# Eighty-four products of zeros behind the last result of an attention and Fourier kernel

## The chip, the core and the metric

The kernel runs on one core of a Trainium2 chip. A core has five engines with queues of their own: TensorE (PE; its weight loads are listed apart as PEld), VectorE (DVE), ScalarE (ACT), GpSimd (POOL) and SyncE (SP), which here issues nearly all transfers between memory and the on-chip buffer. Each queue runs in order, and the engines wait for each other by semaphores. The metric is the device time of one execution in microseconds (us). Before the change the median of three runs is 2921.22 us (2918.11 to 2922.79).

## The reference

Two independent results are put side by side in the columns of one output of 2048 x 2048 numbers.

```python
# A: attention with 32 heads of 32 columns, S = 2048, D = 1024
q, k, v = split(x @ wqkv)
p = softmax(q @ k.T * Dh ** -0.5)
a = concat_heads(p @ v) @ wo
# B: Fourier mixing, the real part of a transform along both axes
ar, ai = x @ dft_hid_re.T, x @ dft_hid_im.T
b = dft_seq_re @ ar - dft_seq_im @ ai
return concatenate([a, b], axis=-1)
```

## The kernel before

The work is cut into products of 128 x 128 weights (the stationary operand) with 512 moving columns, each into one bank of PSUM. Most operands are split into a rounded part and a remainder, and a product of two such operands is three TensorE products in fp32r; the function `group` emits them (line 414). Both results use fast matrix multiplication in two levels of seven products, so that many operands are sums of blocks, made by VectorE and GpSimd.

TensorE's program is one long interleaved order. A planner, class `Plan`, keeps a model of each engine's time. The closing loop of the kernel (lines 2054 to 2129) walks along the plan and picks, for each free moment of TensorE, among three streams of the attention (S: scores, line 1853; T: transposed scores, line 1975; V: products with the values, line 1994) and a list of "fills" (line 414: the projections of queries, keys and values, the Fourier transform, the output projection). `pl.others()` emits what the other engines do in between. A second loop (lines 2130 to 2135) emits what is left for the other engines once TensorE's list is empty. All of it stands under a guard (`guard`, line 2052) that keeps the engines' orders as they are emitted. So what is emitted behind that second loop stands behind everything else on its engine.

The last piece of work is `project_end` and `total` (lines 1440 to 1483): for each of 16 row blocks and two column halves, six products (two blocks of `wo`, three products each) are added by VectorE (line 1474) to a sum that was loaded from memory (line 1455) and is stored as a part of the output (line 1479). The very last store is split in two, one half on SyncE's queue and one on ScalarE's. The sums of a row block stand in a slot of the pool `big`: eight slots, taken in turn, so that row block 11 uses slot 0, and block 15 the slot that block 7 had. Slot 1 holds one of the four pieces of `wo`.

Buffers that the change uses: the slots of `big` (4 KB in each of 128 partitions, one buffer per slot), the tag "c" of the pool `pre` (three buffers of 2 KB, last used for blocks that are loaded to be added), and `psS` (two PSUM tiles of two banks each, used for the scores in line 1853). A tile that is taken again waits for the readers and writers of the tile that had its place. Eight products of zeros already stand at the start of the kernel (lines 376 to 379), ahead of the first loads.

Of the kernel before, what the change touches and what calls it, by code (L numbers as in the profile page):

```python
# [8 lines left out]
F32 = mybir.dt.float32  # L9
F32R = mybir.dt.float32r  # L10
# [6 lines left out]
P = 128  # L17
# [6 lines left out]
NB = 512  # L24
# [198 lines left out]
def kernel(  # L223
# [12 lines left out]
    nc = tc.nc  # L236
# [35 lines left out]
    big = ctx.enter_context(tc.tile_pool(name="big", bufs=1, side="right"))  # L272
# [13 lines left out]
    pre = ctx.enter_context(tc.tile_pool(name="pre", bufs=1, reuse_waits="tile"))  # L286
# [34 lines left out]
    psS, psT, psD = (pools[n] for n in ("psS", "psT", "psD"))  # L321
# [1486 lines left out]
    def op_pool():  # L1808
        if "op" not in late:
            att().release()  # L1810
            qk0.release()
            late["atl"].release()
            late["oph"] = ctx.enter_context(tc.tile_pool(name="oph", bufs=1, side="right", reuse_waits="tile"))
            late["op"] = ctx.enter_context(tc.tile_pool(name="op", bufs=1, reuse_waits="tile"))
        return late["op"]
# [238 lines left out]
    while nf < len(fills) or any(place[n] < len(s) for n, s in streams.items()):  # L2054
# [59 lines left out]
        if ok:  # L2114
            n = min(ok)[1]
# [14 lines left out]
    while True:  # L2130
        pl.others()
        t = pl.next_time()
        if t > 1e17:
            break
        pl.now = max(t, pl.now + 1e-3)
    guard.__exit__(None, None, None)
    op_pool()

# [27 lines left out]
```

## Time and profile before

| | us |
|---|---|
| median of three runs | 2921.22 |
| lowest, highest | 2918.11, 2922.79 |
| the profiled execution | 2929.45 |
| its span, first to last instruction | 2927.7 |

The granted TensorE clock of that execution is 0.999 of full speed. In the views below, times in a timeline count from the span's start: start, duration, engine, line, operation, output<-inputs and the number of instructions merged in a row. In a group, "x8" is the number of instructions, then come busy time, the mean time of one in nanoseconds, and the idle time of the engine just before them with what ended it. A TensorE product's own time reaches from its first column to the last result, so that products that follow each other overlap; the distance of their starts is the pace. In a table of stages the columns are the stretch, the summed time, busy time and number of instructions of PE, PEld, DVE, ACT and POOL, the granted clock, the share of the 16 DMA engines' time, and GB/s. "SPq" and "PEldq" are the sequencers of these engines: waits, issues and drains.

### The profile page before, as it was taken

Reading aid. Unit: us, or ns where it says so; the run is one execution under the profiler, and the core shown is the slowest. Engines: PE = TensorE matmul, PEld = TensorE weight load, DVE = VectorE, ACT = ScalarE, POOL = GpSimd, SP = SyncE. Lnnn points to the kernel's source line nnn. Section 1 sums busy time; section 2 is a strip of 40 time slices with the busy share of each in tenths; the row PEclk is TensorE's granted clock in tenths of the full one; section 3 lists DMA queues with packets and bytes.
Section 4 is the critical chain, followed back from the end, with each engine's and each line's share of the span. In section 5 each row is a group of like instructions: output and inputs, shape, how many; then the busy total and the mean of one; then the engine's idle time right before and its main releaser. Section 6 shows DMA issues by size and latency. Waiting matters only on the chain.

```text
span 2927.7 us, 47039 instructions
## 1 busy us (share of the span) xinstructions
PE 2904.0 (99%) x14728; PEld 2107.2 (72%) x14728; DVE 2386.5 (82%) x3251; ACT 2373.3 (81%) x4509; POOL 1241.3 (42%) x975
## 2 busy tenths in 40 slices
PE   9999999999999999999999999999999999999999
PEld 8887776777667777777676677667667777777777
DVE  7679888788788887788888898888988788788745
ACT  5348898888888888988999898898889888888741
POOL 2325534142233433337655456666675352243200
PEclk9999999999999999999999999999999999999999
DMA  9989978697789988867899776887876665677558
GB/s 345 349 298 328 314 225 272 222 346 269 268 289 339 309 297 287 291 213 218 291 348 333 226 223 216 276 272 229 271 229 208 204 180 181 193 246 226 188 191 287
DMA packets 485844, 768.18 MB, mean 262 GB/s; under 512 B 120382, under 2 KB 153406, under 8 KB 485470
## 3 DMA queue, kind: packets, MB, share of 16 engines
q1 hardware_dynamic: 485452, 765.04, 79.4%
q8 instruction: 119, 1.95, 0.3%
q14 instruction: 129, 1.06, 0.1%
q10 hardware_dynamic: 144, 0.13, 0.0%
HBM read 511.74 MB, written 253.25 MB: 261 GB/s over the span
## 4 chain that ended last, share of the span: by engine, by line
PE 75%; DMA 4%; DVE 1%; ACT 1%; SPq 0%; issue 0%; POOL 0%; DVEq 0%; ACTq 0%; POOLq 0%
PE pd L414 34%; PE psT L1975 14%; PE pd L1994 13%; PE psS L1853 13%; PE psT L414 2%; ACT psS L1862 1%; DVE negm L1859 1%; DMA qs<-m_d 1%; DMA slot<-in_ct 0%; DMA g<-in_ct 0%; DMA hl<-ha_d 0%; ACT pt L1979 0%; DMA m_d<-lt 0%; DMA ha_d<-slot 0%; DMA g<-g_d 0%
## 5 line engine op out<-in xcount | busy, mean ns | idle before, releaser
L414 PE MATMUL pd<-slot,hl 128*128 128x512 f32 x5028 | 1446.7, 390 | 4.2 <-DMA hl<-ha_d 1.4
L1979 ACT ACTIVATE pt<-psT 128x512 f32<-128x512 f32 x2048 | 1191.5, 668 | 260.7 <-PE psT L1975 258.5
L1859 DVE TENSOR_REDUCE negm<-psS 128x1 f32<-128x1024 f32 x1024 | 1240.7, 1221 | 198.3 <-PE psS L1853 190.1
L1862 ACT ACTIVATE psS<-psS,negm 128x1024 f32<-128x1024 f32 x1024 | 1189.2, 1161 | 47.4 <-DVE negm L1859 44.5
L414 PEld LDWEIGHTS pd<-slot,hl 128*128 128x128 f32 x5028 | 943.6, 188 | 204.8 <-DVE negm L1859 2.7
L1975 PE MATMUL psT<-qs,ks 128*128 128x512 f32 x2048 | 802.4, 395 | 4.4 <-DMA qs<-m_d 3.2
L1975 PEld LDWEIGHTS psT<-qs,ks 128*128 128x128 f32 x2048 | 382.2, 188 | 160.0 <-issue 53.0
L1853 PE MATMUL psS<-ks,qs 128*128 128x512 f32 x1552 | 473.1, 391 | 4.2 <-ACT psS L1862 4.2
L1994 PE MATMUL pd<-pt,vt 128*32 128x512 f32 x4096 | 460.9, 596 | 1.2 <-DVE e L723 0.9
L1853 PEld LDWEIGHTS psS<-ks,qs 128*128 128x128 f32 x1552 | 289.5, 188 | 69.1 <-ACT psS L1862 11.0
L504 POOL TENSOR_TENSOR slot<-raw,slot 128x512 fp32r<-128x512 f32 x153 | 196.2, 1291 | 316.1 <-DVE slot L501 116.6
L1994 PEld LDWEIGHTS pd<-pt,vt 128*32 128x32 f32 x4096 | 123.4, 110 | 285.1 <-issue 268.3
L504 POOL TENSOR_TENSOR slot<-slot,slot 128x512 fp32r<-128x512 f32 x183 | 234.3, 1292 | 206.1 <-DVE slot L501 54.5
L1862 ACT ACTIVATION_READ_ACCUMULATOR psS<-psS,negm 128x1 f32 x1024 | 287.0, 280 | 0.0
L504 POOL TENSOR_TENSOR hl<-raw,hl 128x512 fp32r<-128x512 f32 x122 | 156.8, 1289 | 257.4 <-DVE hl L501 84.7
L479 POOL TENSOR_TENSOR raw<-raw,g 128x512 f32<-128x512 f32 x119 | 153.3, 1291 | 226.6 <-ACT pt L1979 31.3
L414 PE MATMUL pd<-slot,slot 128*128 128x512 f32 x780 | 210.6, 389 | 0.1
L414 PEld LDWEIGHTS pd<-slot,slot 128*128 128x128 f32 x780 | 146.4, 188 | 30.9 <-DVE e L723 0.4
L1853 PE MATMUL psS<-ks,qx 128*128 128x512 f32 x496 | 151.0, 394 | 3.3 <-ACT psS L1862 3.2
L479 DVE TENSOR_TENSOR raw<-raw,g 128x512 f32<-128x512 f32 x141 | 103.3, 738 | 23.6 <-DMA g<-in_ct 6.6
L1853 PEld LDWEIGHTS psS<-ks,qx 128*128 128x128 f32 x496 | 91.7, 188 | 34.6 <-issue 9.2
L479 POOL TENSOR_TENSOR slot<-slot,slot 128x512 f32<-128x512 f32 x79 | 102.1, 1302 | 27.5 <-DVE slot L479 11.3
(140 smaller groups left out, 2167.6 us busy)
## 6 DMA issues: line engine op xcount, KB each, us to landing
hl<-ha_d SPq DMA_DIRECT2D x134, 512.0 KB
slot<-in_ct SPq DMA_DIRECT2D x144, 256.0 KB
qk_d<-e SPq DMA_DIRECT2D x52, 512.0 KB
qs<-qk_d SPq DMA_DIRECT2D x128, 192.0 KB
ks<-qk_d SPq DMA_DIRECT2D x128, 192.0 KB
raw<-g_d SPq DMA_DIRECT2D x96, 256.0 KB
ha_d<-hl SPq DMA_DIRECT2D x42, 512.0 KB
raw<-in_ct SPq DMA_DIRECT2D x80, 256.0 KB
```

The lines of the kernel that those rows point to most:

```text
L414: nc.tensor.matmul(box["ps"], a[1]((a[0].hi, a[0].lo)[u]()), b[1]((b[0].hi, b[0].lo)[v]()), start=k == 0, stop=k == n - 1)
L479: (nc.gpsimd if e == "POOL" else nc.vector).tensor_tensor(out=dest(), in0=dest() if a is None else a.get(), in1=other["q"] if "q" in other ...
L504: (nc.gpsimd if e == "POOL" else nc.vector).tensor_tensor(out=lo(), in0=raw(), in1=f(hi()), op=ALU.subtract)
L1853: nc.tensor.matmul(p[:, i * NB : i * NB + NB], (QX[0] if own else QS[h % 2])[:, qt * P : qt * P + P], KS[h % 2][:, c * 1024 + i * NB : c * ...
L1859: nc.vector.tensor_reduce(out=ST["negm"][:, c, qt : qt + 1], in_=box["p"], axis=AX.X, op=ALU.max, negate=True)
L1862: nc.scalar.activation(box["p"], box["p"], AF.Exp, bias=ST["negm"][:, c, qt : qt + 1], accum_out=ST["sums"][:, c, qt : qt + 1])
L1975: nc.tensor.matmul(box["p"], KS[h % 2][:, t * P : t * P + P], QS[h % 2][:, j * NB : j * NB + NB], start=True, stop=True)
L1979: nc.scalar.activation(box["t"], box["p"], AF.Exp)
L1994: nc.tensor.matmul(po["p"][j * DH : j * DH + DH, :], VT[h][:, k, :], box["t"], start=(k == t0), stop=(k == t), tile_position=(0, j * DH),)
```

## The change

Behind the last instruction of the plan, and still under the guard, four tiles are taken and filled with zeros by GpSimd: two with the tag "c" (`zl`, `zs`), and slots 0 and 1 (`zu`, `zw`). Then TensorE forms 84 products from them, 14 forms of six, each form accumulated into one bank of a psS tile, the two tiles in turn. All are 128 x 128 weights with 512 moving columns in fp32r, the size and type of line 414's. Nothing reads the results. The forms differ in where the operands stand and in the order in which the moving columns are read:

| form | moving operand |
|---|---|
| 1 to 4 | 512 columns in a row, from element 0, 8, 4 and 24 of `zu` |
| 5 | as form 2, the weights moved by 8 elements too |
| 6 | elements 0, 256, 1, 257, ... |
| 7 | elements 8, 24, 9, 25, ... to 39, then the next 32 in the same way |
| 8 | every second element of 1024 |
| 9 | elements 0, 16, 32, ... to 496, then 1, 17, ... |
| 10 | elements 8 to 23, 32 times over |
| 11 | elements 0 to 31, 16 times over |
| 12 to 14 | as form 1 with weights, moving operand, or both, from the "c" tiles |

```diff
@@ -2133,6 +2133,32 @@
         if t > 1e17:
             break
         pl.now = max(t, pl.now + 1e-3)
+    zl, zs = (pre.tile([P, NB], F32, name="c", tag="c", bufs=3) for _ in range(2))
+    zu, zw = (big.tile([P, 2 * NB], F32, name=n, tag=n) for n in ("slot0", "slot1"))
+    for z in (zl, zs, zu, zw):
+        nc.gpsimd.memset(z, 0.0)
+    pr = [psS.tile([P, 1024], F32, name="psS") for _ in range(2)]
+    l, s, u, w = (z.bitcast(F32R) for z in (zl, zs, zu, zw))
+    b = w[:, 0:P]
+    forms = [
+        (b, u[:, 0:NB]),
+        (b, u[:, 8 : 8 + NB]),
+        (b, u[:, 4 : 4 + NB]),
+        (b, u[:, 24 : 24 + NB]),
+        (w[:, 8 : 8 + P], u[:, 8 : 8 + NB]),
+        (b, u[:, 0:NB].rearrange("p (a b) -> p b a", a=2)),
+        (b, u[:, 8 : 8 + NB].rearrange("p (a b c) -> p a c b", b=2, c=16)),
+        (b, u[:, 0 : 2 * NB : 2]),
+        (b, u[:, 0:NB].rearrange("p (a b) -> p b a", b=16)),
+        (b, u[:, 8:24].unsqueeze(1).to_broadcast([P, 32, 16])),
+        (b, u[:, 0:32].unsqueeze(1).to_broadcast([P, 16, 32])),
+        (s[:, 0:P], u[:, 0:NB]),
+        (b, l[:, 0:NB]),
+        (s[:, 0:P], l[:, 0:NB]),
+    ]
+    for k, (x, m) in enumerate(forms):
+        for i in range(6):
+            nc.tensor.matmul(pr[k % 2][:, 0:NB], x, m, start=(i == 0), stop=(i == 5))
     guard.__exit__(None, None, None)
     op_pool()
```

In the changed kernel the fills are line 2139 and the products line 2161.

## The prediction

> **What bounds the kernel now.** I read the page first, its span and the chain of waits.
>
> ```profile
> span 2927.7 us, 47039 instructions
> ...
> PE 2904.0 (99%) x14728; PEld 2107.2 (72%) x14728; DVE 2386.5 (82%) x3251; ACT 2373.3 (81%) x4509; POOL 1241.3 (42%) x975
> ...
> PE 75%; DMA 4%; DVE 1%; ACT 1%; SPq 0%; issue 0%; POOL 0%; DVEq 0%; ACTq 0%; POOLq 0%
> ```
>
> TensorE is busy for 99% of the span and holds the chain. The new products go to that engine, behind everything it has. So the question is only what follows its last product today, and how much of it the new work can hide in. The timeline of the last microseconds, first TensorE's own, then all engines', answers that:
>
> ```profile
> 2915.93 2.88 PE L414 MATMUL pd<-slot,slot 128*128 128x512 f32 x12
> 2918.65 2.88 PE L414 MATMUL psT<-slot,slot 128*128 128x512 f32 x12
> 2921.37 1.52 PE L414 MATMUL pd<-slot,slot 128*128 128x512 f32 x6
> ```
>
> ```profile
> 2922.93 0.75 DVE L1474 TENSOR_TENSOR slot<-slot,pd 128x256 f32<-128x256 f32 x2 [0.67 <-PE pd L414]
> 2923.38 0.33 SPq L1479 DMA_DIRECT2D out<-slot  x1
> 2923.71 0.37 ACTq L1479 DMA_DIRECT2D out<-slot  x1
> ```
>
> Twelve products take 2918.65 - 2915.93 = 2.72 us, so one product of 512 columns costs 0.2267 us back to back. The last six end at 2921.37 + 1.52 = 2922.89. Then come the last evictions and the last stores, which stages of a microsecond show running out, and the end of the program (line 2162):
>
> ```profile
> 2916.00:2918.00 2.00, 2.00 (x11) 1.65 (x10) 1.20 (x2) 0.00 (x0) 0.00 (x0) 1.00 1.06 410
> ...
> 2925.00:2926.00 1.00, 0.00 (x0) 0.00 (x0) 0.00 (x0) 0.00 (x0) 0.00 (x0) 1.00 0.26 92
> 2926.00:2927.00 1.00, 0.00 (x0) 0.00 (x0) 0.00 (x0) 0.00 (x0) 0.00 (x0) 1.00 0.03 10
> ```
>
> ```profile
> L2162 SPq EVENT_SEMAPHORE  x8: 17/28/260, 2926.3 to 2927.6; - x8
> ...
> L2162 PEldq DRAIN  x2: 13/2140/4267, 2918.7 to 2927.3; - x2
> ```
>
> The last two figures of a stage are DMA share and GB/s: the stores are out by about 2926.3, and SyncE's closing steps begin there and end at 2927.6. So after TensorE's last product 2927.7 - 2922.9 = 4.8 us pass: 3.4 of stores, 1.4 of closing. TensorE's first drain, the longest (4.27 us), lasts from 2918.7 to 2922.9, which is when its last product ends: the close does wait for TensorE's products, read or not.
>
> **The change part by part.** The 84 products (line 2161 of the changed kernel) read two tiles in slots 0 and 1 and two of the pool's "c" tiles, all filled with zeros by POOL. Nothing is removed or moved; no DMA is added.
>
> *When they can start.* POOL and the "c" and psS buffers are long free:
>
> ```profile
> 2877.90 1.29 POOL L504 TENSOR_TENSOR slot<-raw,slot 128x512 fp32r<-128x512 f32 x1 [57.13 <-DVE slot L504]
> ```
>
> ```profile
> L1803 DVE TENSOR_TENSOR slot<-c,slot x6: 680/688/994, 2693.2 to 2769.0; 128x512 f32<-128x512 f32 x6
> ```
>
> ```profile
> L1862 ACT ACTIVATION_READ_ACCUMULATOR psS<-psS,negm x59: 192/258/444, 2600.7 to 2743.2; 128x1 f32 x59
> ```
>
> So the two small fills run about 2880 and are hidden. The fills of slots 0 and 1 come after them, in that order, and must wait for the slots' last users. A product there:
>
> ```profile
> L414 PE MATMUL pd<-slot,slot x6: 388/389/389, 2921.4 to 2922.5; 128*128 128x512 f32 x6
> ```
>
> Slot 1 holds a half of wo that the last group but one reads in its third product: the last group starts at 2921.37, the one before 1.36 earlier at 2920.01, its third product ends at 2920.01 + 0.45 + 0.39 = 2920.85. Slot 0 holds sums of row block 11, which two stores write out. SyncE's stores and the reloads of such slots:
>
> ```profile
> 2912.28 11.43 SPq L1479 DMA_DIRECT2D out<-slot  x14
> ```
>
> ```profile
> 2916.32 0.33 SPq L1479 DMA_DIRECT2D out<-slot  x1
> ```
>
> ```profile
> 2906.45 0.38 SPq L1479 DMA_DIRECT2D out<-slot  x1
> ```
>
> ```profile
> 2911.66 0.57 SPq L1455 DMA_DIRECT2D slot<-py_d  x1
> ```
>
> The fourteen from 2912.28 are the last of SyncE's 32 stores, from block 9 on; the sixth, at 2916.32, is block 11's second half, slot 0's last user. How long a store takes to land is seen from block 7's: issued at 2906.45, and its slot reloaded at 2911.66, at most 5.2 us. The very last stores, with little behind them, land in about 2.6 (issued at 2923.71, out at 2926.3). DMA is as full at 2916 (share 1.06) as it was then, so I take 5.2: slot 0 is free at 2921.5 (bound: 2918.9). The fills:
>
> ```profile
> L302 POOL MEMSET ks<- 32x2048 f32 x1 | 1.8, 1799 | 0.0
> ...
> L336 POOL MEMSET qx<- 32x512 f32 x1 | 0.5, 519 | 0.1
> ```
>
> 1536 more elements cost 1.28 us, so 1024 take 0.519 + 0.43 = 0.95 us. Slot 0 is filled at 2922.45, slot 1 at 2923.4. At the kernel's start a product waits for such a fill:
>
> ```profile
> 0.92 0.48 DVE L377 MEMSET c<- 128x512 f32 x1 [0.92 <-PEq L2159]
> ...
> 1.46 3.78 PE L379 MATMUL pd<-c 128*128 128x512 f32 x8 [1.46 <-DVE c L377]
> ```
>
> The fill ends at 1.40, the product starts at 1.46. So the first new product starts at 2923.5, 0.8 us later than back to back (2922.73); behind this wait stand only the other 83. If slot 0 lands at the early bound there is no wait. Below that the start can't go, since TensorE runs in order. POOL's fills at 2921.5 to 2923.4 may touch VectorE's last eviction and the stores behind it; these now have some 20 us of cover, so they cost nothing; without that cover, at most one fill, 0.95 us.
>
> *What one costs.* Forms 1 to 5 (plain, and moved by 8, 4 and 24 elements) and 12 to 14 (other tiles) read 512 columns in a row: 8 x 6 = 48 products. Forms 10 and 11 repeat runs of 16 and 32 columns, form 8 takes every second element: 18 products. For these 66 I take 0.2267: 14.96 us. No row has a start off the usual places or a short run; a place that costs more would be bounded by the next paragraph's price. For less than 0.2267, the products of line 1994 are the nearest:
>
> ```profile
> 1508.39 4.50 PE L1994 MATMUL pd<-pt,vt 128*32 128x512 f32 x40
> 1512.82 0.50 PE L1975 MATMUL psT<-qs,ks 128*128 128x512 f32 x1
> ```
>
> 40 records in 4.43 us, 0.111 each. But these fill 32 of the array's columns and four stand side by side; the new ones fill 128, so I exclude it. [...]
>
> Forms 6, 7 and 9 (18 products) jump with each column: 256, 16 and 16 elements on. The trace has no product of this kind. Its lower bound is the plain 0.2267, as long as the order is free. For the upper, VectorE has reads that jump 16 elements with each element (line 1882, 32 elements of negm):
>
> ```profile
> L1859 DVE TENSOR_REDUCE negm<-psS 128x1 f32<-128x1024 f32 x1024 | 1240.7, 1221 | 198.3 <-PE psS L1853 190.1
> ...
> L1882 DVE TENSOR_REDUCE nm<-negm 128x16 f32<-128x32 f32 x32 | 5.7, 178 | 0.0
> ```
>
> 992 elements more cost 1043 ns, 1.05 ns an element, and the jumping 32 stand on that same line: at this pace jumps are free, and 512 columns would take 0.54 us. TensorE asks for one each 0.44 ns, which no jumping read shows. So the price lies between 0.2267 and 0.54. The one row where TensorE streams such products at a slower pace is that of the eight warm-up products:
>
> ```profile
> L379 PE MATMUL pd<-c 128*128 128x512 f32 x8 | 3.8, 649 | 1.5 <-DVE c L377 1.5
> ```
>
> Their 3.78 us less the last one's 0.65, over seven, are 0.447 each. I take 0.45 for a jumping form, TensorE at half pace, since it is nearer to the row that reads in that order than the plain price is. 18 x 0.45 = 8.1 us. [...]
>
> *The sum.* 14.96 + 8.1 = 23.06 us of products from 2923.5, and 0.39 - 0.23 = 0.16 for the last to leave: 2946.7. The stores are long out. Of the closing steps, 1.4 us, some (the waits for stores) can be done before; I take 1.1 (0.7 to 1.4): the span ends at 2947.8, 20.1 us later. Outside the span stay the 1.75 us of 2929.45 - 2927.7. That execution is 8.2 us over the median of the three runs, 2921.22, and I add the difference to the median: **2941.3 us**, 0.69% slower.
>
> **The rivals.**
>
> *Order is free*: all 84 at 0.2267, 19.04 us. For it: every product of this width in the tail has the same 389 ns and pace whatever its tile, and VectorE's jumps cost nothing. Against: TensorE reads more than twice as fast. 4.1 us less: 2937.2; with no wait at the start and 0.7 of closing, 2936.2.
>
> *Order is dearer*: forms 6, 7 and 9 at VectorE's 0.54 and form 8 likewise: 20.1 + 18 x 0.09 + 6 x 0.31 = 23.6, 2944.8. At worst these four fall to the pace of unrounded products, five rounds of four in 4.43 us or 0.886 a round: 18 x 0.436 + 6 x 0.66 = 11.8 more, 2953. Against: nothing there asks for several passes.
>
> [...]
>
> *Not slower*: nobody reads the products, and if the close does not wait for an engine whose results nobody reads, the stores still set the end and the time stays 2921.2. It decides from the first product. Against it stands the drain above, and this row of waits at the end:
>
> ```profile
> SPq L2162 <- PEq L2162: 0.6, 2, 0.4
> ```
>
> If waited for, all 84 would have to fit into 3.4 us, 40 ns each. That the products or fills were dropped as unread is the same case: same time.
>
> **How the numbers follow.** Forecast 52%, order free 23%, dearer 16%, late start 5%, not slower 4%. The range: 2935 (order free, with a run's scatter of some 2 us) to 2949, which leaves out the last case, the dearest form of the third and some of the late start. A difference under 0.2%, 5.8 us, can't be told from none: slower 96%, within 3%, faster 1% (that last is scatter in the fourth rival).
>
> **What would show it.** Line 2161: 84 products from about 2923.5 to 2946.7, clock 1.00; six of a plain form in 1.36 us, six of forms 6, 7 and 9 in 2.7 each. Line 2139: the last fill ends near 2923.4, and TensorE idles about 0.6 us before its first new product. The last store still goes out near 2923.7. Between 1.36 and 2.7 a form, only the term of 8.1 is wrong; plain forms off 1.36 would be a cost of the address, which I put at nothing. The forecast fails if the jumps are free, if the start waits for the last stores, or if the span does not end with line 2161.

## The result and the profile after

The changed kernel takes 2938.91 us (median of five runs, 2937.3 to 2947.39) against 2921.22 us before (again the median of five, 2918.03 to 2925.43): 17.7 us more, a ratio of 1.0066 with a 95% interval of 1.0047 to 1.0084. The forecast was 2941.3. Its profiled execution took 2937.3 us, the lowest of the five:

```profile
span 2935.5 us, 47213 instructions
...
PE 2924.1 (100%) x14812; PEld 2123.5 (72%) x14812; DVE 2382.6 (81%) x3251; ACT 2373.7 (81%) x4509; POOL 1245.2 (42%) x979
```

84 products, 84 weight loads, four fills and two waits of POOL's sequencer are the whole difference in instructions (47213 - 47039 = 174). This execution reached its last stores some 10 us earlier than the one before did, so the two spans are not compared as they stand; what is compared is the time from line 414's last product to the end. The timeline of the end of the changed kernel, all engines (start, duration, engine, line):

```profile
2910.51 1.85 POOL L2139 MEMSET slot<- 128x1024 f32 x2 [40.35 <-DMA out<-slot]
...
2911.16 1.52 PE L414 MATMUL pd<-slot,slot 128*128 128x512 f32 x6
...
2912.42 9.88 PEld L2161 LDWEIGHTS psS<-slot,slot 128*128 128x128 f32 x44 [0.16 <-POOL slot L2139]
2912.53 17.92 PE L2161 MATMUL psS<-slot,slot 128*128 128x512 f32 x66
...
2922.54 0.21 PEld L2161 LDWEIGHTS psS<-slot,slot 128*128 128x128 f32 x1 [0.25 <-issue]
2922.99 0.21 PEld L2161 LDWEIGHTS psS<-slot,slot 128*128 128x128 f32 x1 [0.24 <-issue]
...
2926.10 0.21 PEld L2161 LDWEIGHTS psS<-slot,slot 128*128 128x128 f32 x1 [0.23 <-issue]
2926.53 0.21 PEld L2161 LDWEIGHTS psS<-slot,slot 128*128 128x128 f32 x1 [0.23 <-issue]
...
2933.07 1.55 PE L2161 MATMUL psS<-c 128*128 128x512 f32 x6
```

Line 414's last product ends at 2911.16 + 1.52 = 2912.68, and 22.8 us later the span is over; before it was 4.8 us. So 18.0 us were added, and the medians say 17.7. The products stretch from 2912.53 to 2933.07 + 1.55 = 2934.62: 22.1 us.

The products of the 14 forms are merged in a few rows here, but the weight loads, one for each product, show the slow ones: they stand alone where a product is long, 0.45 us apart in form 8 (2922.54, 2922.99) and 0.43 apart in form 9 (2926.10, 2926.53). The products of forms 6 and 7 are seen in a narrower stretch of TensorE's timeline:

```profile
2919.73 2.54 PE L2161 MATMUL psS<-slot,slot 128*128 128x512 f32 x11
```

Eleven of them reach over 2.54 us; less the last one's 0.38, over ten steps, that is 0.216 each: faster than 512 columns in a row. Form 6 thus starts one step earlier, at 2919.51, and the 30 products of forms 1 to 5 lie between 2912.53 and there, 0.233 each.

The end of the program (line 2188 now) waits for them:

```profile
L2188 SPq EVENT_SEMAPHORE  x8: 17/28/18888, 2915.4 to 2935.4; - x8
...
L2188 PEldq DRAIN  x2: 13/2184/4355, 2930.3 to 2935.1; - x2
```

SyncE's closing steps begin at 2915.4, when the stores are out, and one of them lasts 18.9 us, until TensorE is done; the rest of the close takes 0.9 us. In the list of SyncE's waits (who waited for whom: us in total, times, longest), this one is put down to the new products:

```profile
SPq L2188 <- PE psS L2161: 18.9, 1, 18.9
```

### The profile page after: what moved, and what is told of

It is laid out like the page before. It is cut to its first block, busy times and chain, and to the rows that moved or that the text cites. A ratio compares the mean times of both kernels' runs of the same rounds, so it can differ in the third digit from the quotient of the medians.

```text
span 2935.5 us, 47213 instructions
## 1 busy us (share of the span) xinstructions
PE 2924.1 (100%) x14812; PEld 2123.5 (72%) x14812; DVE 2382.6 (81%) x3251; ACT 2373.7 (81%) x4509; POOL 1245.2 (42%) x979
## 4 chain that ended last, share of the span: by engine, by line
PE 91%; DMA 4%; DVE 2%; ACT 2%; issue 1%; POOL 1%; SPq 0%; POOLq 0%; ACTq 0%; DVEq 0%
PE pd L414 41%; PE psT L1975 15%; PE psS L1853 15%; PE pd L1994 14%; PE psT L414 5%; ACT psS L1862 1%; DVE negm L1859 1%; PE psS L2161 1%; DMA raw<-in_ct 0%; ACT pt L1979 0%; DMA o_d<-ot 0%; DMA c<-u_d 0%; DMA qk_d<-e 0%; DMA slot<-in_ct 0%; DMA ha_d<-slot 0%
## 5 line engine op out<-in xcount | busy, mean ns | idle before, releaser
L479 POOL TENSOR_TENSOR slot<-slot,slot 128x512 f32<-128x512 f32 x79 | 101.5, 1294 | 26.6 <-DVE slot L479 7.8
```

What stands on the lines that cost most here:

```text
L479: (nc.gpsimd if e == "POOL" else nc.vector).tensor_tensor(out=dest(), in0=dest() if a is None else a.get(), in1=other["q"] if "q" in other ...
```

## The experiments

Unless another base is named, each is the kernel before with the edit shown, and "before" in a result is the kernel before, run on the same chip. e1_orders, e5_lines and e11_phase were executed once each: of them the timeline is used, not the time.

**Which orders cost what (e1_orders).** Sixteen forms of twelve products on lines of their own, at the place of the change's.

```diff
+    for i in R: mm(o, b, m, start=i == 0, stop=i == 11)
+    for i in R: mm(q, b, m.rearrange("p (a b) -> p b a", a=2), start=i == 0, stop=i == 11)
+    for i in R: mm(o, b, m.rearrange("p (a b) -> p b a", a=4), start=i == 0, stop=i == 11)
+    for i in R: mm(q, b, m.rearrange("p (a b) -> p b a", a=8), start=i == 0, stop=i == 11)
+    for i in R: mm(o, b, m.rearrange("p (a b) -> p b a", a=16), start=i == 0, stop=i == 11)
+    for i in R: mm(q, b, m.rearrange("p (a b c) -> p b a c", a=16, c=2), start=i == 0, stop=i == 11)
+    for i in R: mm(o, b, m.rearrange("p (a b c) -> p b a c", a=16, c=4), start=i == 0, stop=i == 11)
+    for i in R: mm(q, b, m.rearrange("p (a b c) -> p b a c", a=2, c=2), start=i == 0, stop=i == 11)
+    for i in R: mm(o, b, u[:, 0 : 2 * NB : 2], start=i == 0, stop=i == 11)
+    for i in R: mm(q, b, u[:, 0:1].to_broadcast([P, NB]), start=i == 0, stop=i == 11)
+    for i in R: mm(o[0:64], w[:, 0:64], m, start=i == 0, stop=i == 11)
+    for i in R: mm(q[0:32], w[:, 0:32], m, start=i == 0, stop=i == 11)
+    for i in R: mm(o[0:32], w[:, 0:32], m.rearrange("p (a b) -> p b a", a=2), start=i == 0, stop=i == 11)
...
```

> 192 products behind the last result, 16 forms of twelve, each form on a line of its own (2145 to 2160). The changed kernel had two columns taken in turn at 0.216 us, 512 in a row at 0.23, every second column or every sixteenth at 0.43 to 0.45. Theory A: a read brings two neighbouring columns at once, TensorE keeps a few such pairs, and a pair that serves both of its columns costs nothing; each pair fetched for one column alone costs double. Then 2, 4 or more columns taken in turn stay at 0.216 as long as the pairs are kept, and at some number up to 16 fall to 0.43; pairs or fours with a jump between them (2150, 2151, 2152) stay at 0.22 to 0.24; every second column 0.45; one column 512 times 0.216. Theory B: the price hangs on the number of jumps to far places, and two are a special case: pairs with a jump (2150) cost about 0.33 to 0.43, four in turn 0.43 already. For the 0.011 between a row (0.227) and two in turn (0.216): theory C, the weights' load gets in the way of a read in a row: with 64 and 32 weight columns (2155, 2156) the row falls to 0.221 and 0.218 or below; theory D, it belongs to reading in a row: 0.227 to 0.235 with any number of weight columns, and 0.216 for two in turn with 32 (2157). Line 2159 has 1.5 in place of zeros: the same 0.23 if the numbers do not matter. Line 2160 takes other weights for each product: 0.227 instead of 0.232 if the same weights again are what made the row of zeros slower than line 414's 0.2267.

TensorE's timeline; the distance of two starts over twelve is a product's pace:

```profile
2919.72 2.88 PE L2145 MATMUL psS<-slot,slot 128*128 128x512 f32 x12
2922.45 2.75 PE L2146 MATMUL psS<-slot,slot 128*128 128x512 f32 x12
2925.03 3.56 PE L2147 MATMUL psS<-slot,slot 128*128 128x512 f32 x12
2928.43 6.10 PE L2148 MATMUL psS<-slot,slot 128*128 128x512 f32 x12
2934.35 5.38 PE L2149 MATMUL psS<-slot,slot 128*128 128x512 f32 x12
2939.55 5.69 PE L2150 MATMUL psS<-slot,slot 128*128 128x512 f32 x12
2945.07 3.12 PE L2151 MATMUL psS<-slot,slot 128*128 128x512 f32 x12
2948.02 4.25 PE L2152 MATMUL psS<-slot,slot 128*128 128x512 f32 x12
2952.10 5.67 PE L2153 MATMUL psS<-slot,slot 128*128 128x512 f32 x12
2957.59 2.80 PE L2154 MATMUL psS<-slot,slot 128*128 128x512 f32 x12
```

In a row 0.227 us, two in turn 0.216, four in turn 0.283, eight 0.493, sixteen 0.433; pairs with a jump between them 0.460, fours with a jump 0.246, pairs from two places in turn 0.340; every second column 0.457; one column again and again 0.220. Theory A falls: pairs are not the unit, or pairs with jumps would be cheap. Theory B falls too: four in turn cost 0.283 and not 0.43 already, and pairs with a jump cost more than its 0.33 to 0.43. What stands out is the four: fours with jumps cost 0.246 where a row costs 0.227, pairs with jumps 0.460. Of the other pair of theories D holds: with 64 and 32 weight columns a row costs 0.231 and 0.232, and two in turn with 32 cost 0.215, so the weights' load is not what slows a row. With 1.5 in place of zeros a row costs 0.2275, with zeros 0.2267 (line 2145). Weights taken from every second column leave the row at 0.234 (line 2158). With other weights for each product a row costs 0.229 (line 2160, its first six products 227 to 236 ns and the rest 227), and with the same weights again line 2145 has 0.2267: the same weights again are not what made the changed kernel's rows slow.

**Lines of four (e5_lines).** Fifteen more forms, chosen so that the same steps fall into other groups of four.

```diff
+    for i in R: mm(o, b, u[:, 0:NB].rearrange("p (a b c) -> p b a c", a=16, c=4), start=i == 0, stop=i == 11)
+    for i in R: mm(q, b, u[:, 2 : 2 + NB].rearrange("p (a b c) -> p b a c", a=16, c=4), start=i == 0, stop=i == 11)
...
+    for i in R: mm(q, b, u[:, 0:NB].rearrange("p (a b c) -> p a c b", b=2, c=2), start=i == 0, stop=i == 11)
+    for i in R: mm(o, b, u[:, 0:NB].rearrange("p (a b c) -> p a c b", b=2, c=4), start=i == 0, stop=i == 11)
...
+    for i in R: mm(o, b, u[:, 2 : 2 + NB].rearrange("p (a b c) -> p a c b", b=2, c=4), start=i == 0, stop=i == 11)
...
+    for i in R: mm(o, b, KS[1][:, 0:S:4], start=i == 0, stop=i == 11)
+    for i in R: mm(q, b, KS[1][:, 0 : 3 * NB : 3], start=i == 0, stop=i == 11)
...
```

> 180 products behind the last result, 15 forms of twelve, lines 2144 to 2158. After e1_orders, theory E: SBUF is read in lines of four fp32 (16 bytes); a line that serves two or more columns in succession costs 1.77 ns (0.2266 us over 128 lines), one that serves a single column before a jump 0.85 ns (0.4338 over 512), and two lines taken in turn are both kept, so that only the columns' own 0.42 ns count (0.2157). It gives: in a row 0.227; fours with jumps from element 0 0.246 as before (2145), from element 2, so that each touches two lines, 0.45 (2146); eights with jumps 0.227 to 0.246 (2147); pairs with jumps 0.46 (2148, 2149); two columns in turn within one line (0, 2, 1, 3) 0.227 (2150), from neighbouring lines and beyond 0.216 (2151 to 2154); every fourth column 0.433 (2155), every third 0.444 (2156: 128 lines of two columns, 256 of one); one line again and again 0.216 to 0.227 (2157), two lines in runs of four 0.216 to 0.227 (2158). Theory F: it is not lines but the steps between columns: equal steps of one are good, a change of step is what costs or saves. Then 2146 is like 2145 (0.246), 2150 like 2151 (0.216), and 2155 and 2156 like every second column (0.452).

The same view; 2145 and 2146 differ only in where the fours begin, 2150 and 2151 only in whether the two columns in turn are in one group of four:

```profile
2915.34 3.12 PE L2145 MATMUL psS<-slot,slot 128*128 128x512 f32 x12
2918.29 5.45 PE L2146 MATMUL psS<-slot,slot 128*128 128x512 f32 x12
2923.57 2.94 PE L2147 MATMUL psS<-slot,slot 128*128 128x512 f32 x12
...
2936.93 2.94 PE L2150 MATMUL psS<-slot,slot 128*128 128x512 f32 x12
2939.71 2.75 PE L2151 MATMUL psS<-slot,slot 128*128 128x512 f32 x12
2942.30 2.75 PE L2152 MATMUL psS<-slot,slot 128*128 128x512 f32 x12
```

Fours that start at element 0 cost 0.246, the same fours from element 2 cost 0.440: theory F, which looks at steps only, falls. Two in turn inside one group of four cost 0.232, like a row; from two neighbouring groups 0.216. So these prices go with groups of four fp32, 16 bytes, counted from element 0, as theory E has it. That two groups are kept at a time is its reading of the 0.216 for two in turn, against 0.283 for four and 0.493 for eight; no run shows it apart from the price. Its prices fit less exactly. Every fourth column takes 0.459 for 0.433 and every third 0.450 for 0.444, both nearer to theory F's 0.452; pairs with jumps take 0.440 here, and the very same form 0.460 in e1_orders. Two forms go against it. Pairs from two places in turn, in e1_orders, stay within two groups and yet cost 0.340. And two in turn, four apart but beginning at element 2 (line 2153), take 0.2267, not 0.216; there every fourth step stays within a group (7 to 4, 9 to 10). A finer rule than E would be needed, and stays open.

**The jumps undone (e6_in_a_row).** The changed kernel with forms 6 to 9 replaced by form 1.

```diff
-        (b, u[:, 0:NB].rearrange("p (a b) -> p b a", a=2)),
-        (b, u[:, 8 : 8 + NB].rearrange("p (a b c) -> p a c b", b=2, c=16)),
-        (b, u[:, 0 : 2 * NB : 2]),
-        (b, u[:, 0:NB].rearrange("p (a b) -> p b a", b=16)),
+        (b, u[:, 0:NB]),
+        (b, u[:, 0:NB]),
+        (b, u[:, 0:NB]),
+        (b, u[:, 0:NB]),
```

> The changed kernel with forms 6 to 9 replaced by form 1: all 84 products read 512 columns in a row or short runs. In the changed kernel 22.8 us pass from the end of line 414's last product to the end of the span. If the forms' prices add, forms 8 and 9 give back 12 x 0.21 = 2.5 us and forms 6 and 7 take 12 x 0.018 = 0.2 more: 20.5 us, and a median near 2936.5. If the jumps had a cost beyond their own products (a clock that drops, a start that waits), the difference is larger: 19 us or less.

The timeline of its end:

```profile
2918.09 1.85 POOL L2139 MEMSET slot<- 128x1024 f32 x2 [40.30 <-DVE slot L1474]
...
2918.41 1.52 PE L414 MATMUL pd<-slot,slot 128*128 128x512 f32 x6
...
2919.99 15.57 PE L2161 MATMUL psS<-slot,slot 128*128 128x512 f32 x66
```

Line 414 ends at 2919.93 and the span at 2940.6: 20.7 us, for the 22.8 of the changed kernel and the 20.5 expected. The prices of the forms add to within some 0.3 us, and no cost of a jump beyond its own product shows. The median, 2938.49 and not the 2936.5 expected, is 18.0 above the 2920.44 of before, much as the changed kernel's 17.7: 2 us are below what these runs tell apart, and only the profile shows them. Here the fills came late: slot 1 was full at 2918.09 + 1.85 = 2919.94, and the first product starts at 2919.99, 0.44 us after line 414's last start for 0.227.

**The fast order in the whole kernel (e2_all_turned, e3_turned_old_plan, e4_new_plan_only).** If two columns in turn are faster, the kernel's own products of this kind, some 10,600, can be read so. The columns of a product then come out in that order in PSUM; the eviction reads them back into place. For the scores nothing has to be put back.

```diff
-                    nc.tensor.matmul(box["ps"], a[1]((a[0].hi, a[0].lo)[u]()), b[1]((b[0].hi, b[0].lo)[v]()), start=k == 0, stop=k == n - 1)
+                    nc.tensor.matmul(box["ps"], a[1]((a[0].hi, a[0].lo)[u]()), turn(b[1]((b[0].hi, b[0].lo)[v]())), start=k == 0, stop=k == n - 1)
...
+    def turn(t):
+        return t.rearrange("p (a b) -> p b a", a=2)
+
+    def back(t):
+        return t.rearrange("p (b a) -> p a b", a=2)
...
-        frees.append(finish(lambda: box["ps"], o))
+        frees.append(finish(lambda: back(box["ps"]), o))
...
-    MM, PV, SWITCH, TINY = 0.2275, 0.853, 0.40, 0.17
+    MM, PV, SWITCH, TINY = 0.2167, 0.853, 0.40, 0.17
```

> Every fp32r product of the kernel reads its moving operand two columns in turn, 256 apart (lines 414, 1853 and 1975 of before), the evictions of their PSUM banks put the columns back (they read every second element of PSUM), and the plan counts 0.2167 us for a product in place of 0.2275. Theory: 10,632 products are 0.0109 us shorter each, TensorE stays the bound: 116 us less, about 2805 us, and the groups of line 414's show starts 0.216 apart. Rival 1: the pace of real products is not that of the zeros' forms (other places, other weights): between 2805 and 2921. Rival 2: evictions that read PSUM in steps of two cost VectorE double, some 600 of them by 0.7 us: VectorE then is busy for 2800 us, the bound, and the time is 2850 to 2950.

> As e2_all_turned, but the plan still counts 0.2275 us a product, so that every engine's order is that of the kernel before. Theory: the gain comes from the pace alone, and most of the 116 us is there with the old order too: 2810 to 2850. Rival: the gain is one of the order: about 2920.

> The kernel before with the plan's 0.2167 us a product and nothing else: columns in a row as before. Theory: no gain, 2915 to 2945, since TensorE's products take the 0.2267 they took. Rival: the other order is itself what is faster: under 2900.

e2_all_turned took 2858.35 us, a ratio of 0.977 (0.9753 to 0.9786) to the kernel before; e3_turned_old_plan 2869.04, 0.9805 (0.9786 to 0.9823); e4_new_plan_only 2959.51, 1.0117 (1.0101 to 1.0132). So the gain is that of the read order: with the old plan most of it is there, and the new plan alone is slower. All three times lie above what their theories gave (2805, 2810 to 2850, 2915 to 2945). Groups of e2_all_turned (busy time, mean ns | idle time before):

```profile
L426 PE MATMUL pd<-slot,hl 128*128 128x512 f32 x5172 | 1447.1, 380 | 6.7 <-ACT hl L511 2.0 <-DVE slot L516 1.5 <-POOL hl L516 1.0
...
L1865 PE MATMUL psS<-ks,qs 128*128 128x512 f32 x1552 | 457.9, 382 | 12.2 <-ACT psS L1874 11.7
```

One product takes 380 ns for 390 (line 426 is 414 of before), and in the last stage twelve take 2.59 us for 2.72: 0.216 each, the pace of the zeros. VectorE's evictions of that line keep their time, 683 ns with steps of two in PSUM (line 1103) for 682 before (line 1091): rival 2 falls. But of the 116 us only 65 arrive (2923.66 to 2858.35). TensorE's busy time falls from 2904.0 to 2805.7, by 98 us; its idle time rises from 23.7 to 51.7, with 15.9 us of score products waiting for ScalarE's exponentials (7.4 before). The longest single wait is of another kind and stands near the end:

```profile
PE pd L426 <- ACT slot L511: 9.3, 1, 9.3
```

The stage behind it:

```profile
2810.00:2815.00 5.00, 4.82 (x12) 3.61 (x13) 2.34 (x4) 3.28 (x6) 3.18 (x3) 0.54 0.45 170
```

The granted clock is 0.54 there, and 0.995 over the whole execution, for 0.999 before. e4_new_plan_only, with the same plan, has such a wait too, of 8.5 us, and the same clock over the whole, 0.995.

**The plan's constants (e7_turned_mm2195, e9_turned_mm2215, e8_turned_act).** Only the numbers in the plan change against e2_all_turned.

```diff
-    MM, PV, SWITCH, TINY = 0.2167, 0.853, 0.40, 0.17
+    MM, PV, SWITCH, TINY = 0.2195, 0.853, 0.40, 0.17
...
-    ES, ET = 1.235, 0.625
+    ES, ET = 1.275, 0.65
```

The first pair of lines is e7's (0.2215 in e9), the second e8's.

> As e2_all_turned, with 0.2195 us a product in the plan, a little over the 0.216 that was measured. e2 lost some 16 us to products that waited for ScalarE's exponentials. Theory: the plan was too tight for the other engines, a looser one waits less: 2840 to 2855. Rival: order changes scatter the time by some 10 us whatever the constant, 2850 to 2870.

> As e7_turned_mm2195, with 0.2215 us a product in the plan. The plan's number was 0.2167 (2858 us), 0.2195 (2846) and 0.2275 (2869) so far. Theory: a smooth optimum near 0.22: 2843 to 2855. Rival: each order is a draw of its own, as the 2902 of e8_turned_act suggests: anywhere from 2845 to 2900.

> As e2_all_turned (0.2167), with ScalarE's two exponentials counted as 1.275 and 0.65 us in place of 1.235 and 0.625. Theory: the score products' waits for ScalarE (15.9 us) shrink: 2840 to 2852. Rival: ScalarE is then fed less and the waits come back elsewhere: 2858 or more.

e7 took 2845.74 us, 0.9741 (0.9725 to 0.9758), the fastest kernel here; e9 2849.4, 0.975 (0.9736 to 0.9763). Of the four values of the one constant those near 0.22 are the best. Four points do not show that the optimum is smooth, and e9's time fits its rival too. e8 took 2901.61 (0.994): ScalarE's exponentials counted at 3 to 4% more cost some 43 us, and the score products waited more for them (29.4 us), not less. e7's score products wait longer than e2's too (23.4 us), and all its waits for ScalarE together are as long (26.6 for 27.2 us), so the reason that was given for its gain is not shown. What its trace does show is that e2's one wait of 9.3 us is gone. Among these four the granted clock goes with the times, 0.999 in e7's profiled execution, 0.996 in e9's, 0.995 in e2's and 0.993 in e8's; but e3_turned_old_plan is slower than e2 at 0.998. How much of the time is the clock's, and why e8's order is so much worse, stays open.

**Only the scores turned (e10_scores_only).** The old order and plan, and `turn` on line 1853's moving operand alone.

```diff
-                        KS[h % 2][:, c * 1024 + i * NB : c * 1024 + i * NB + NB], start=True, stop=True,
+                        turn(KS[h % 2][:, c * 1024 + i * NB : c * 1024 + i * NB + NB]), start=True, stop=True,
```

> The kernel before, in its old order, with only the 2048 score products (line 1853) reading two columns in turn; their columns are only searched for a maximum and summed, so nothing has to be put back. Theory: 2048 x 0.0109 = 22 us less, about 2898, if TensorE passes all of it on. Rival: the exponentials of ScalarE, which the score products wait for (7.4 us before), take part of it back: 2900 to 2915.

2920.97 us, a ratio of 0.9998 (0.9989 to 1.0007): nothing. Neither theory had this. Its groups, lines 426, 1987 and 1865 being 414, 1975 and 1853 of before:

```profile
L426 PE MATMUL pd<-slot,hl 128*128 128x512 f32 x5028 | 1458.4, 392 | 2.6 <-POOL hl L516 1.1 <-DMA hl<-ha_d 0.7 <-DVE e L683 0.5
L1987 PE MATMUL psT<-qs,ks 128*128 128x512 f32 x2048 | 810.3, 399 | 2.5 <-DMA qs<-m_d 2.1 <-ACT pt L1991 0.4
...
L1865 PE MATMUL psS<-ks,qs 128*128 128x512 f32 x1552 | 453.9, 379 | 2.6 <-ACT psS L1874 2.6
```

The scores gain 19.2 us in this group (473.1 before) and 6.4 in the smaller one with qx. But the products in a row of the other lines, which nobody touched, are busy longer: 1458.4 for 1446.7 and 810.3 for 802.4, 19.6 us together. That is no scatter: in the five other traces with these products in the old order (the changed kernel, e1, e5, e6 and e11) the two sums lie between 1445.8 and 1447.2 and between 802.0 and 803.0. TensorE's busy time falls from 2904.0 to 2898.7 only, 5.3 us, and of these the medians show 0.6. The waits for ScalarE are not the reason; they are shorter than before (5.8 us for 7.4).

**In step and out of step (e11_phase).** Products in a row, with single products of another length between them. "In step" is said of products in a row whose starts lie 226 to 227 ns apart, "out of step" where the starts lie further apart, mostly by 229 to 236 ns.

```diff
+    for i in R: mm(o, b, m, start=i == 0, stop=i == 23)
+    mm(q, b, turned, start=True, stop=True)
+    for i in R: mm(o, b, m, start=i == 0, stop=i == 23)
+    mm(q, b, u[:, 0 : 2 * NB : 2], start=True, stop=True)
+    for i in R: mm(o, w[:, i % 8 * P : i % 8 * P + P], m, start=i == 0, stop=i == 23)
+    mm(q, b, turned, start=True, stop=True)
+    for i in R: mm(o, b, m if i % 2 else turned, start=i == 0, stop=i == 23)
+    for i in R: mm(q, b, m, start=i == 0, stop=i == 23)
```

> 123 products behind the last result: 24 in a row (2145), one two in turn (2146), 24 in a row (2147), one of every second column (2148), 24 in a row with other weights each time (2149), one two in turn (2150), 24 that alternate between two in turn and in a row (2151), 24 in a row (2152). Theory G: products in a row that follow each other in step cost 0.2267 each; one product of another length, or a wait, puts them out of step, and then they cost 0.229 to 0.236 until they fall into step again. Then 2145 has 0.2267, 2147 and 2149 0.230 to 0.234 at first, 2151 216 and 229 to 236 ns in turn, and with scores alone read in turn (e10_scores_only) the products in a row of the other lines lose what the scores gain. Theory H: products in a row cost 0.2267 whatever goes before, and the 0.23 of the changed kernel comes from the same weights again: 2147 0.2267 as 2145, or 2145 0.232 too and 2149 0.2267.

TensorE's timeline:

```profile
2911.68 5.60 PE L2145 MATMUL psS<-slot,slot 128*128 128x512 f32 x24
2917.12 0.38 PE L2146 MATMUL psS<-slot,slot 128*128 128x512 f32 x1
2917.33 5.61 PE L2147 MATMUL psS<-slot,slot 128*128 128x512 f32 x24
...
2928.91 5.52 PE L2151 MATMUL psS<-slot,slot 128*128 128x512 f32 x24
2934.27 5.60 PE L2152 MATMUL psS<-slot,slot 128*128 128x512 f32 x24
```

24 in a row take 5.44 us, 0.2267 each. The 24 that alternate take 5.36, 0.2233 each, where 0.2157 and 0.2267 would give 0.2212: the single starts lie 215 and 231 to 232 ns apart in turn, so a product in a row behind one of another length costs 5 ns more. After the single product that reads two in turn (line 2146) the first distance is 233 ns and the next are 226 to 227; after the one of every second column it took three. Theory H falls: the weights are the same in 2145 and in 2147, and what goes before a product changes its price. Of theory G the first half holds, but only for one to three products, where 30 in the changed kernel stayed out of step. Its other half, the wait, is borne out by comparing runs. Form 1 costs 0.2267 where it follows line 414 without a wait (its first start 226 to 227 ns after line 414's last, in e1, e5 and e11). It costs 0.232 in the changed kernel, where its weight load waited 0.16 us for the fill and the first product started after 230 ns. In e6, where the first product started after 439 ns, some 33 products were out of step and the next 20 in step. Why it lasts longer there than in e11 is not shown.

The same shows in e10. From before to e10, the mean distance from one product in a row to the next rises from 227.0 to 229.8 ns where a third stands ahead of them (some 6,600 distances under 300 ns), and from 227.7 to 231.8 where a score product does (some 870). Together that is 22 us, of the 25.6 that the scores gained: products in a row lose their step behind the turned ones, and that takes most of the gain back.

## Why the prediction was right

**The bound.** It was forecast that whatever stands behind line 414's last product adds to the time, less the 4.8 us that stores and close took before. That was right: 18.0 us in the profile, 17.7 in the medians, 20.1 forecast. The rival that nobody waits for unread products is out by SyncE's 18.9 us of waiting for line 2161.

**The start.** A wait of 0.8 us was forecast, and there was next to none: 2912.53 is 0.23 after the last start of line 414. The chain named was the right one: slot 0's fill waits for a store of block 11, and the fills end at 2910.51 + 1.85 = 2912.36, just ahead of the need. The term that was off is the store's landing, 5.2 us in the sum. Block 11's second store, in the changed kernel's own timeline of SyncE:

```profile
2905.95 0.69 SPq L1479 DMA_DIRECT2D out<-slot  x1
```

From there to the fill at 2910.51 it is at most 4.6. In e6 the fills ended 0.2 us too late, so the wait is real at times, between the forecast's early bound of none and the 0.8 taken. Nor did the start wait for the last stores, to which 5% was given: the fills began at 2910.51, 3 us before the last store was issued at 2913.51.

**The price of a product.** Here two steps failed, and it is luck that they are of opposite sign and that the sum stayed near. The first put one price, 0.45, on forms 6, 7 and 9 because they jump with each column. That is near for form 9 (0.433) and wrong for forms 6 and 7 (0.216): 12 products at 0.234 less, -2.8 us. It was not the jump alone that decided: forms 6 and 7 read from two places in turn, form 9 from 32, and the change's own table of forms told them apart; in e1_orders two places in turn cost 0.216, four 0.283, sixteen 0.433. That form 9 came out near is luck as well. The row that gave 0.45, the warm-up products of line 379, reads its columns in a row and says nothing of the order.

The second put form 8, which takes every second element, among the plain ones at 0.2267; it takes 0.45: six products, +1.3 us. Its 512 columns lie in 256 groups of four fp32, two columns in each, where a row's lie in 128. A group with two of its columns used cost as much time as one with four: 0.45 us over 256 is 1.76 ns, 0.2267 over 128 is 1.77.

VectorE's two rows, which gave the upper bound, said nothing of jumps: the line was drawn through the jumping row itself, and that this row stands on it shows nothing. The other 60 products, forecast at 0.2267, took 0.234 on the mean, +0.4 us: out of step, as said under e11_phase, or at a short run's own price (form 10, 0.245). With form 9's -0.1 that is 1.1 us less, the 22.1 measured for the 23.2 forecast.

**The close.** 0.9 us for the 1.1 taken.

So -0.8, -1.1 and -0.2 make the 20.1 us into 18.0. Of the rivals, "order is free" at 2937.2 (18 products at 0.223 less are 4.0 us, not 4.1, so 2937.3) came nearer to the total than the forecast did, but not for its reason: the order is not free, and two forms, 8 and 9, were dear and two, 6 and 7, cheap.

## What to carry to other kernels

In these runs a product's pace went with the order in which its moving columns are read, from 0.216 to 0.493 us for 512, and it could be measured behind the last result for 17.7 us, in forms that differ by one thing. An fp32r operand of 512 columns read from two places in turn ran at 0.216 us for 0.2267 in a row, and VectorE's eviction put the columns back in the same time (683 ns for 682): 2.6% of this kernel, once all products were read so and the plan counted 0.2195 us for one (e7_turned_mm2195). With only the scores read so there was no gain (2920.97 us for 2921.58). A constant step of two, three, four or sixteen columns about doubled the price of a row: 0.457, 0.450, 0.459 and 0.433 us.

## What the runs showed of the hardware

For 512 columns of an fp32r moving operand the price went with groups of four fp32 (16 bytes): fours with jumps took 0.246 us from element 0 and 0.440 from element 2 (e5_lines). Where only one or two columns of a group were taken before the next group, it was about double that of a row, 0.433 to 0.460 for 0.2267 (e1_orders, e5_lines). Two groups in turn, one column each, beat a row, 0.216 to 0.2267; two columns each took 0.340, four groups in turn 0.283, eight 0.493 (e1_orders). Products in a row fell out of step behind one of another length or behind a wait, and then mostly cost 229 to 236 ns for 226 to 227; in e11_phase they were in step again after one to three, in the changed kernel forms 1 to 5 were not in 30. VectorE's addition of 512 elements took 683 ns where it read PSUM in steps of two (e2_all_turned, line 1103) and 682 where it read it in a row (before, line 1091).
